# Decode attention with an FFN gate: 4-byte transposes, the FFN in column tiles in mid-stream, and a new order of loads

## Chip, cores and metric

The kernel runs on one core of one Trainium2 chip. The metric is the device time of one execution in microseconds. "Before" is the kernel as it stood, "after" the changed one. Runs differ in state: a run more than 1.5% above the fastest of the same kernel counts as slow. Ratios are the mean time of one kernel's fast runs over that of the other's of the same rounds, so they are not quite the ratio of the medians that I quote.

## The reference

Two batch rows, one new token each. The only large inputs are the last 2048 rows of the K and V caches (8 heads, 256 wide, 16 query heads), `wq`, `wo`, and the FFN's `w1` and `w2`.

```python
xn = layernorm(x)                                  # x: [2, 1, 448]
q  = (xn @ wq) as [2, 16 heads, 1, 256]
k, v = last 2048 rows of the caches, each of 8 heads used by 2 query heads
s  = softmax(q k^T / 16) v, as [2, 1, 4096] @ wo
g  = silu(relu(xn @ w1) @ w2)                      # w1: [448, 1792]
out = x + s * g                                    # bf16
```

## The kernel before

One pair is one of the 8 K/V heads for both batch rows: 2 MB of K and 2 MB of V (MB here is 2^20 bytes), in rows interleaved by batch over 128 partitions. A pair is cut into 8 steps. Step i transposes a chunk of K on TensorE into one of three PSUM banks, and VectorE (even i) or ScalarE (odd i) evacuates it, that is, copies it to SBUF. Scores, softmax and PV products (softmax weights times V) of earlier pairs stand between the steps.

```python
def do_T(i):                                       # one of 64 steps
    k, s = divmod(i, NCH)
    bank, src = tb[i % 3], kbuf[k % NKB]
    deps = [*d_k[k], p_id, evac.get(i - 3)]
    for n in range(8):
        lo = (4 * s + n % 4) * DH + 128 * (n // 4)
        o = pr.op(PE, lambda e, n=n, lo=lo: e.matmul(
            bank[:, n * 128:(n + 1) * 128], lhsT=src[:, lo:lo + 128], rhs=ident[:, :],
            start=True, stop=True, is_transpose=True), deps)
    ...
    if i % 2 == 0:
        evac[i] = pr.op(DVE, lambda e: e.tensor_copy(dst, bank[:, :]), deps)
    else:
        evac[i] = pr.op(ACTE, lambda e: e.activation(dst, bank[:, :], ACT.Copy), deps)

# pair k, e = 8k: scores at steps e+8, e+9; softmax e+9 to e+15 (row sum "ch_sum" at e+15);
# PV at e+17 to e+24; o_sb, oT after that.
# ... cut
order = ["v0"] + [n for k in range(2, NPAIR - 2) for n in (f"k{k}", f"v{k - 1}")]
order += ["k6", "k7", "v5", "v6", "v7"]            # k0, wq, k1 come first
# ... cut
load_w1(0)
load_w2(0)
# wo in four parts: 16, 10, 4, 2 of 32 slots; all the loads on one queue
do_H(0); do_H(1)                                   # h = relu(x w1): 2 x 7 products, 4 x 448 out
do_hT()
# ... at2: the attention output, folded for wo
do_F()                                             # h w2, then silu: ScalarE exp, VectorE 3 ops
# 128 products with wo, then out = x + s * g
```

Below, Kn and Vn are the K and V of pair n; H are the products with w1, hT the transposes of their result, F the products with w2. PE is TensorE, and a "row sum" is the small product `ch_sum`: that of one pair's softmax closes the next pair's transposes, so row sums mark TensorE's pace.

## Time and profile before

| | before |
|---|---|
| median, range | 115.96 us, 115.94 to 118.28 (3 runs) |
| profiled run | 118.03 us, span 114.7 us, slow |
| moved | 44.3 MB (decimal), 386 GB/s over the span |
| TensorE, VectorE, ScalarE busy | 74%, 41%, 40% |
| transposes (bf16, 512) | 42.0 us busy |

The page cuts the span into 40 slices; a digit is a busy share in tenths. The chain of waits lists what ended last, in time order, as start, duration, what. A full DMA row tells that transfers never stop; it does not tell that they set the end. For that, look at the last lines of the chain. Here TensorE stands there. The lines themselves are in the prediction below.

### The profile page before, as it was taken

The page shows a single profiled execution, that of the slowest core. Times are in us where ns is not written, and L with a number is a line of the kernel's source. Part 1 is how long each engine was busy: PE and PEld are TensorE (multiplying, and loading weights), DVE is VectorE, ACT ScalarE, POOL GpSimd, SP SyncE. Part 2 cuts the span into 40 slices and gives each one's busy share as a digit, 9 for nine tenths or more (in the row PEclk, how much of TensorE's full clock was granted, in tenths as well). Part 3 has the DMA queues.
Part 4 walks back from the last instruction along what each step waited for, and adds up shares of the span by engine and source line. Part 5 has one row for each costly group of instructions (what it writes and reads, how often), then busy time and mean ns, then how long its engine had stood idle before and what let it go on. Part 6 is the DMA issues. An engine that isn't in the chain of part 4 may idle for free.

```text
span 114.7 us, 2834 instructions
## 1 busy us (share of the span) xinstructions
PE 85.0 (74%) x1262; PEld 56.1 (49%) x1262; DVE 46.6 (41%) x123; ACT 45.7 (40%) x56; POOL 1.8 (2%) x13
## 2 busy tenths in 40 slices
PE   0009906089569989986998996799899858777890
PEld 0009902056444765753576574466576525212870
DVE  2633503025422636633454754464574513222231
ACT  1903630006953493490358358168358140000000
POOL 6000000000000000000000000000000000000000
PEclk9999999959976999998599999999999995555559
DMA  4899989999999999999999999999999999999300
GB/s 92 366 434 480 450 373 434 383 457 446 388 446 446 383 446 440 400 434 440 400 431 428 411 434 423 428 423 417 440 417 411 415 415 417 451 402 401 133 0 3
DMA packets 3744, 44.28 MB, mean 386 GB/s; under 512 B 659, under 2 KB 789, under 8 KB 1173
## 3 DMA queue, kind: packets, MB, share of 16 engines
q1 hardware_dynamic: 3704, 44.11, 91.7%
q8 instruction: 9, 0.15, 0.5%
q14 instruction: 3, 0.02, 0.0%
q10 hardware_dynamic: 28, 0.00, 0.0%
HBM read 44.11 MB, written 0.00 MB: 384 GB/s over the span
## 4 chain that ended last, share of the span: by engine, by line
PE 43%; DMA 41%; DVE 5%; SPq 4%; issue 3%; ACT 1%
DMA kbuf<-in_A_k_cache_dram 41%; PE tb L268 16%; PE sbk L249 8%; PE obk L249 7%; PE fbk L249 6%; PE mbk L249 6%; SPq L36 4%; DVE o_sb L353 1%; DVE h_n L400 1%; ACT e_sb L318 1%; DVE pt L330 1%; PE mbk L304 1%; DVE rm L299 1%; DVE tmp L496 0%; DVE out_sb L498 0%
## 5 line engine op out<-in xcount | busy, mean ns | idle before, releaser
L268 PE MATMUL tb<-ident,kbuf 128*128 128x128 bf16 x512 | 42.0, 235 | 9.1 <-issue 5.9
L281 ACT ACTIVATE kt<-tb 128x1024 bf16<-128x1024 bf16 x32 | 31.8, 1021 | 38.9 <-PE tb L268 38.9
L268 PEld LDWEIGHTS tb<-ident,kbuf 128*128 128x128 bf16 x512 | 33.4, 105 | 16.4 <-issue 14.0
L279 DVE COPY kt<-tb 128x1024 bf16<-128x1024 bf16 x32 | 22.1, 690 | 23.6 <-PE tb L268 23.5
L249 PE MATMUL obk<-vbuf,pt 128*4 128x256 bf16 x256 | 17.8, 295 | 0.0
L318 ACT ACTIVATE e_sb<-sbk,bias 128x1024 bf16<-128x1024 f32 x8 | 8.9, 1114 | 7.2 <-DVE bias L314 7.1
L249 PE MATMUL sbk<-kt,qz 128*4 128x512 bf16 x128 | 11.7, 443 | 0.0
L249 PEld LDWEIGHTS obk<-vbuf,pt 128*4 128x4 bf16 x256 | 6.0, 86 | 6.1 <-issue 0.6
L299 DVE TENSOR_REDUCE rm<-sbk 128x1 f32<-128x512 f32 x8 | 5.5, 692 | 7.8 <-PE sbk L249 7.8
L249 PE MATMUL fbk<-w_sb,xr 128*4 128x448 bf16 x14 | 5.5, 572 | 0.7 <-DVE h_n L400 0.7
L420 ACT ACTIVATE ea<-fbk 128x112 f32<-128x112 f32 x1 | 0.3, 263 | 14.4 <-PE fbk L249 14.4
L249 PE MATMUL mbk<-ssum,gsum 128*128 128x1 f32 x16 | 3.3, 273 | 3.1 <-DVE pt L330 1.9
L330 DVE TENSOR_TENSOR pt<-mbk,par 128x128 bf16<-128x128 f32 x8 | 2.3, 292 | 6.5 <-PE mbk L249 6.5
L353 DVE TENSOR_SCALAR o_sb<-obk,rs 128x256 bf16<-128x256 f32 x8 | 3.9, 484 | 2.3 <-PE obk L249 2.3
L249 PE MATMUL mbk<-ident,e_sb 128*128 128x16 bf16 x64 | 2.9, 171 | 2.4 <-ACT e_sb L318 2.4
L249 PEld LDWEIGHTS mbk<-ssum,gsum 128*128 128x128 f32 x16 | 2.6, 203 | 3.8 <-DVE pt L330 3.8
L249 PE MATMUL mbk<-ident,xg 2*128 2x2 bf16 x7 | 0.3, 163 | 5.5 <-DVE xg L228 5.5
L249 PEld LDWEIGHTS mbk<-ident,e_sb 128*128 128x128 bf16 x64 | 2.1, 96 | 3.5 <-ACT e_sb L318 2.8
L249 PE MATMUL obk<-wqo,xr 128*4 128x512 bf16 x28 | 1.7, 379 | 2.7 <-DMA wqo<-in_A_wq_dram 2.7
L249 PE MATMUL sbk<-wqo,at 128*2 128x112 bf16 x128 | 3.4, 297 | 0.2 <-issue 0.2
L249 PEld LDWEIGHTS fbk<-w_sb,xr 128*4 128x4 bf16 x14 | 1.5, 115 | 4.0 <-issue 2.5
L400 DVE TENSOR_SCALAR h_n<-fbk 4x448 bf16<-4x448 f32 x2 | 1.2, 612 | 5.3 <-PE fbk L249 5.3
(61 smaller groups left out, 43.8 us busy)
## 6 DMA issues: line engine op xcount, KB each, us to landing
kbuf<-in_A_k_cache_dram SPq DMA_DIRECT2D x16, 1024.0 KB, 19.9
vbuf<-in_A_v_cache_dram SPq DMA_DIRECT2D x16, 1024.0 KB, 22.6
wqo<-in_A_wq_dram SPq DMA_DIRECT2D x1, 3584.0 KB, 14.9
w_sb<-in_B_w_dram SPq DMA_DIRECT2D x2, 1568.0 KB, 22.5
wqo<-in_A_wo_dram SPq DMA_DIRECT2D x1, 1792.0 KB, 27.9
wqo<-in_A_wo_dram SPq DMA_DIRECT2D x1, 1120.0 KB, 30.2
wqo<-in_A_wo_dram SPq DMA_DIRECT2D x1, 448.0 KB, 29.9
wqo<-in_A_wo_dram SPq DMA_DIRECT2D x1, 224.0 KB, 30.0
```

What stands on the lines that cost most here:

```text
L36: o = _Op(eng, lambda e: e.dma_start(dst, src), [d for d in deps if d is not None], True)
L249: return lambda e: e.matmul(out_ap, lhsT=lhsT, rhs=rhs, start=start, stop=stop, skip_group_check=True, **kw)
L268: o = pr.op(PE, lambda e, n=n, lo=lo: e.matmul(bank[:, n * 128:(n + 1) * 128], lhsT=src[:, lo:lo + 128], rhs=ident[:, :], start=True, stop ...
L279: evac[i] = pr.op(DVE, lambda e: e.tensor_copy(dst, bank[:, :]), deps)
L281: evac[i] = pr.op(ACTE, lambda e: e.activation(dst, bank[:, :], ACT.Copy), deps)
L299: st["rm", k] = pr.op(DVE, lambda e: e.tensor_reduce(out=rm[k % 2][:, :], in_=sbk[:, :], axis=AX.X, op=ALU.max), [st["S", k], st.get(("rmT ...
L304: st["rmT", k] = pr.op(PE, lambda e: e.matmul(mbk_ap(0, 128, 1), lhsT=rm[k % 2][:, :], rhs=ident_f[:, :], start=True, stop=True, is_transp ...
L318: st["exp", k] = pr.op(ACTE, lambda e: e.activation(view(e_sb[k % 2], 0, [[2, 512], [1, 2]]), view(sbk, 0, [[1, 512], [0, 2]]), ACT.Exp, b ...
L330: st["pt", k] = st["mbk"] = pr.op(DVE, lambda e: e.tensor_tensor(out=view(pt[k % NP], 0, [[4, 32], [2, 2], [1, 2]]), in0=view(mbk, 256, [[ ...
L353: st["osb", k] = pr.op(DVE, lambda e: e.tensor_scalar(out=o_sb[k % 2][:, :], in0=obk[k % 2][:, 0:DH], scalar1=rs[:, k:k + 1], scalar2=None ...
L400: st["h_n"] = pr.op(DVE, lambda e: e.tensor_scalar(out=h_n[0:4, u * (FC // 2):(u + 1) * (FC // 2)], in0=fbk[0:4, 0:FC // 2], scalar1=0.0, ...
L420: a_e = pr.op(ACTE, lambda e: e.activation(ea[:, :], fbk[:, 0:NCOL], ACT.Exp, scale=-1.0), [o])
```

## The change

It has four parts. (1) K is transposed as 4-byte elements, half as many products, and the evacuation sorts the result by batch and parity with a strided read. (2) The FFN is computed in four column tiles and in pair 5 instead of in the tail. (3) w1 and w2 are loaded among the K/V pairs, k7 behind v5, wo last. (4) The first K pair comes in halves on two queues, with x behind it. The intent is to take the FFN out of the tail and halve the count of transposes.

```diff
+        d_k[0] = {}
+        for h in range(2):
+            for b in range(2):
+                lo = h * (NT // 2) * DH
+                d_k[0][h, b] = pr.dma((SP, ACTE)[b] if h == 0 else SP, ...)
+        d_x = pr.dma(ACTE, x_sb[0:B, :], A_x[:, 0, :])      # was first
...
-            for n in range(8):
-                lo = (4 * s + n % 4) * DH + 128 * (n // 4)
+            for n in range(4):
+                lo = (4 * s + n) * (DH // 2)
                 o = pr.op(PE, lambda e, n=n, lo=lo: e.matmul(
-                    bank[:, n * 128:(n + 1) * 128], lhsT=src[:, lo:lo + 128], rhs=ident[:, :],
+                    bank_f[:, n * 128:(n + 1) * 128], lhsT=src_f[:, lo:lo + 128], rhs=ident_f[:, :],
...
-                evac[i] = pr.op(DVE, lambda e: e.tensor_copy(dst, bank[:, :]), deps)
+                evac[i] = pr.op(DVE, lambda e: e.tensor_copy(dst, view(bank, 0, [[1, 4], [4, 256]])), deps)
             else:                                           # ScalarE likewise
...
-                o = pr.op(PE, mm(fbk[0:4, 0:FC // 2], xr[:, 4 * s:4 * s + 4], w1_sb[:, lo:lo + FC // 2], ...
+                for i in range(4):
+                    o = pr.op(PE, mm(fbk[32 * i:32 * i + 4, 0:256], xr[:, 4 * s:4 * s + 4],
+                                     view(w1_sb, s * FC + min(2 * i, 5), [[7, 128], [1, 2]]),
+                                     s == 0, s == SLOTS - 1, tile_position=(0, 32 * i)), deps)
...
+        at_step(5 * NCH + 2, 6, do_H)
+        at_step(5 * NCH + 4, 6, do_hT)
+        at_step(5 * NCH + 6, 6, do_F)
...
-        order += ["k6", "k7", "v5", "v6", "v7"]
+        for n in "v0 k2 v1 k3 v2 w1 k4 v3 w2 k5 v4 k6 v5 k7 v6 v7".split():
```

More of the change, by code (lines that the diff above doesn't have):

```diff
@@ L142, in bass_recurrent_scan__sliding_block_cached__dense_activation_relu__decode_kernel @@
         qz = named("qz", [128, 16 * NPAIR], BF)
-        h_n = named("h_n", [128, FC], BF)
+        h_n = named("h_n", [128, 256], BF)
         h_sb = named("h_sb", [128, 28], BF)
@@ L182, in kv_dst @@
             return view(t, 0, [[1, NT * DH]], n=64, p0=b, pstep=2)
-        d_x = pr.dma(ACTE, x_sb[0:B, :], A_x[:, 0, :])
         p_xc = pr.op(POOL, lambda e: e.memset(x_c[:, :], 0.0))
-        d_xc = [pr.dma(ACTE, view(x_c, 0, [[1, NCOL]], n=4, p0=b, pstep=32),
-                       A_x[b, 0, :].rearrange("(i n) -> i n", i=4), [p_xc]) for b in range(B)]
         d_k, d_v = {}, {}
@@ L202, in load_v @@
                       for b in range(2)]
-        load_k(0)
+        d_k[0] = {}
+        for h in range(2):
+            for b in range(2):
+                lo = h * (NT // 2) * DH
+                d_k[0][h, b] = pr.dma((SP, ACTE)[b] if h == 0 else SP,
+                                      view(kbuf[0], lo, [[1, NT // 2 * DH]], n=64, p0=b, pstep=2),
+                                      kv_src(0, b, A_k_cache)[:, lo:lo + NT // 2 * DH])
+        d_x = pr.dma(ACTE, x_sb[0:B, :], A_x[:, 0, :])
+        d_xc = [pr.dma(ACTE, view(x_c, 0, [[1, NCOL]], n=4, p0=b, pstep=32),
+                       A_x[b, 0, :].rearrange("(i n) -> i n", i=4), [p_xc]) for b in range(B)]
         d_wq = pr.dma(SP, wqo[:, 0:SLOTS * HC], wq_src)
@@ L250, in mm, with do_xr @@
                                       skip_group_check=True, **kw)
-        for s in range(SLOTS):
-            m_xr = pr.op(PE, mm(mbk_ap(2 * s, 2), xg[0:B, 128 * s + 128:128 * s + 256], ident[0:B, 0:B], s == 0),
-                         [v_xn, p_id])
-        v_xr = pr.op(DVE, lambda e: e.tensor_tensor(
-            out=view(xr, 0, [[4, SLOTS], [2, 2], [1, 2]]), in0=view(mbk, 0, [[2, SLOTS], [0, 2], [1, 2]]),
-            in1=view(par8, 0, [[1, SLOTS], [1, 2], [0, 2]]), op=ALU.mult), [m_xr, v_par8])
+        def do_xr():
+            for s in range(SLOTS):
+                m_xr = pr.op(PE, mm(mbk_ap(2 * s, 2), xg[0:B, 128 * s + 128:128 * s + 256], ident[0:B, 0:B], s == 0),
+                             [v_xn, p_id])
+            st["xr"] = pr.op(DVE, lambda e: e.tensor_tensor(
+                out=view(xr, 0, [[4, SLOTS], [2, 2], [1, 2]]), in0=view(mbk, 0, [[2, SLOTS], [0, 2], [1, 2]]),
+                in1=view(par8, 0, [[1, SLOTS], [1, 2], [0, 2]]), op=ALU.mult), [m_xr, v_par8])
         evac, last_S, freed = {}, {}, set()
@@ L264, in do_T @@
             bank, src = tb[i % 3], kbuf[k % NKB]
-            deps = [*d_k[k], p_id, evac.get(i - 3)]
-            for n in range(8):
-                lo = (4 * s + n % 4) * DH + 128 * (n // 4)
+            src_f, bank_f = src[:, :].bitcast(F32), bank[:, :].bitcast(F32)
+            landed = [d_k[0][s // 4, b] for b in range(2)] if k == 0 else d_k[k]
+            deps = [*landed, p_idf, evac.get(i - 3)]
+            for n in range(4):
+                lo = (4 * s + n) * (DH // 2)
                 o = pr.op(PE, lambda e, n=n, lo=lo: e.matmul(
-                    bank[:, n * 128:(n + 1) * 128], lhsT=src[:, lo:lo + 128], rhs=ident[:, :],
+                    bank_f[:, n * 128:(n + 1) * 128], lhsT=src_f[:, lo:lo + 128], rhs=ident_f[:, :],
                     start=True, stop=True, is_transpose=True), deps)
@@ L278, in do_T @@
             if i % 2 == 0:
-                evac[i] = pr.op(DVE, lambda e: e.tensor_copy(dst, bank[:, :]), deps)
+                evac[i] = pr.op(DVE, lambda e: e.tensor_copy(dst, view(bank, 0, [[1, 4], [4, 256]])), deps)
             else:
-                evac[i] = pr.op(ACTE, lambda e: e.activation(dst, bank[:, :], ACT.Copy), deps)
+                evac[i] = pr.op(ACTE, lambda e: e.activation(dst, view(bank, 0, [[1, 4], [4, 256]]), ACT.Copy), deps)
         def do_S(k, b):
@@ L289, in do_S @@
                     o = pr.op(PE, mm(sbk[32 * i:32 * i + 4, :], lhsT,
-                                     view(kt[(ch // 2) % (NKT // 2)], 512 * dhi + b, [[1024, 2], [2, 256]]),
+                                     view(kt[(ch // 2) % (NKT // 2)], 256 * (2 * b + dhi), [[1024, 2], [1, 256]]),
                                      b == 0 and dhi == 0, b == 1 and dhi == 1, tile_position=(0, 32 * i)),
@@ L370, in do_q @@
         def do_q():
-            deps = [d_wq, v_xr, a_z[0]]
+            deps = [d_wq, st["xr"], a_z[0]]
             for s in range(SLOTS):
@@ L380, in do_q @@
                 out=q_n[:, :], in0=obk[0][:, :], scalar1=SCALE, scalar2=None, op0=ALU.mult), [o])
-            deps = [v, v_xr]
+            deps = [v, st["xr"]]
             for n in range(4):
                 o = pr.op(PE, lambda e, n=n: e.matmul(
-                    mb16[:, 128 * n:128 * n + 128], lhsT=q_n[:, 128 * n:128 * n + 128],
+                    mb16[:, 128 * n:128 * n + 128], lhsT=view(q_n, 256 * (n // 2) + n % 2, [[2, 128]]),
                     rhs=ident[:, :], start=True, stop=True, is_transpose=True), deps)
@@ L391, in do_q, with do_H @@
                         view(mb16, 256 * r + b, [[2, 2], [32, 4], [128, 2]])), [o, p_qz])
-        def do_H(u):
-            deps = [st["w1"], a_z[3], st.get("h_n")]
+        def do_H():
+            deps = [st["w1"], st["xr"], a_z[3]]
             for s in range(SLOTS):
-                lo = s * FC + u * (FC // 2)
-                o = pr.op(PE, mm(fbk[0:4, 0:FC // 2], xr[:, 4 * s:4 * s + 4], w1_sb[:, lo:lo + FC // 2],
-                                 s == 0, s == SLOTS - 1), deps)
-                deps = []
+                for i in range(4):
+                    o = pr.op(PE, mm(fbk[32 * i:32 * i + 4, 0:256], xr[:, 4 * s:4 * s + 4],
+                                     view(w1_sb, s * FC + min(2 * i, 5), [[7, 128], [1, 2]]),
+                                     s == 0, s == SLOTS - 1, tile_position=(0, 32 * i)), deps)
+                    deps = []
             st["h_n"] = pr.op(DVE, lambda e: e.tensor_scalar(
-                out=h_n[0:4, u * (FC // 2):(u + 1) * (FC // 2)], in0=fbk[0:4, 0:FC // 2],
+                out=view(h_n, 0, [[1, 128], [128, 2]]), in0=view(fbk, 0, [[2, 128], [1, 2]]),
                 scalar1=0.0, scalar2=None, op0=ALU.max), [o])
@@ L405, in do_hT @@
             deps = [st["h_n"]]
-            for j in range(7):
-                o = pr.op(PE, mm(fbk[:, 4 * j:4 * j + 4], view(h_n, j, [[7, 128]], n=4), ident[0:4, 0:4], j == 0), deps)
+            for jj in range(2):
+                o = pr.op(PE, mm(fbk[:, 256 + 16 * jj:272 + 16 * jj], h_n[:, 128 * jj:128 * jj + 128],
+                                 view(ident, 0, [[32, 4], [1, 4]]), True, True), deps)
                 deps = []
+            for jj in range(2):
+                st["hT"] = pr.op(DVE, lambda e, jj=jj: e.tensor_copy(
+                    view(h_sb, 2 * jj, [[4, 3], [14, 2], [1, 2]]), view(fbk, 256 + 16 * jj, [[4, 3], [2, 2], [1, 2]])), [o])
             st["hT"] = pr.op(DVE, lambda e: e.tensor_copy(
-                view(h_sb, 0, [[2, 7], [14, 2], [1, 2]]), view(fbk, 0, [[4, 7], [2, 2], [1, 2]])), [o])
+                view(h_sb, 12, [[14, 2], [1, 2]]), view(fbk, 284, [[2, 2], [1, 2]])), [o])
         def do_F():
@@ L439, in bass_recurrent_scan__sliding_block_cached__dense_activation_relu__decode_kernel @@
             at_step(i, 0, lambda i=i: do_T(i))
+        at_step(2, 1, do_xr)
         at_step(NCH - 1, 1, do_q)
+        at_step(5 * NCH + 2, 6, do_H)
+        at_step(5 * NCH + 4, 6, do_hT)
+        at_step(5 * NCH + 6, 6, do_F)
         for k in range(NPAIR):
@@ L454, in bass_recurrent_scan__sliding_block_cached__dense_activation_relu__decode_kernel @@
             at_step(e + 25, 5, lambda k=k: do_oT(k))
-        order = ["v0"] + [n for k in range(2, NPAIR - 2) for n in (f"k{k}", f"v{k - 1}")]
-        order += ["k6", "k7", "v5", "v6", "v7"]
         loads = []
-        for n in order:
-            load, nb = (load_k, NKB) if n[0] == "k" else (load_v, NVB)
-            loads.append((load, int(n[1]), nb))
+        for n in "v0 k2 v1 k3 v2 w1 k4 v3 w2 k5 v4 k6 v5 k7 v6 v7".split():
+            if n[0] == "w":
+                loads.append(((load_w1, load_w2)[int(n[1]) - 1], 0, 1))
+            else:
+                load, nb = (load_k, NKB) if n[0] == "k" else (load_v, NVB)
+                loads.append((load, int(n[1]), nb))
         for i in range(max(steps) + 1):
@@ L468, in bass_recurrent_scan__sliding_block_cached__dense_activation_relu__decode_kernel @@
         assert not loads
-        load_w1(0)
-        load_w2(0)
         d_wo = []
@@ L476, in bass_recurrent_scan__sliding_block_cached__dense_activation_relu__decode_kernel @@
             j0 += n
-        do_H(0)
-        do_H(1)
-        do_hT()
         for b in range(2):
@@ L485, in bass_recurrent_scan__sliding_block_cached__dense_activation_relu__decode_kernel @@
                 view(at2, b, [[2, 32]]), mbk_ap(256 + 32 * b, 32)), [m_at])
-        do_F()
         deps = [v_at2, st["exp", NPAIR - 1]]
```

## The prediction

> **What bounds it now.** I first read the page's slices. The DMA row stands at 9 from the third slice to the 37th, so all but the ends is a full transfer stream; the TensorE clock falls to half for the last seven slices.
>
> ```profile
> PE   0009906089569989986998996799899858777890
> PEclk9999999959976999998599999999999995555559
> DMA  4899989999999999999999999999999999999300
> ```
>
> The table of windows says how steady the stream is, and where it ends: 421 to 434 GB/s through the middle, a ragged end, nothing after 109 us.
>
> ```profile
> 72.00:82.00 10.00, 9.20 (x147) 6.11 (x147) 5.24 (x13) 5.08 (x6) 0.00 (x0) 1.00 1.01 426
> 82.00:92.00 10.00, 9.30 (x153) 6.10 (x146) 5.61 (x17) 5.08 (x6) 0.00 (x0) 1.00 1.01 425
> 108.00:109.00 1.00, 1.00 (x54) 1.00 (x49) 0.25 (x2) 0.26 (x1) 0.00 (x0) 0.50 0.05 16
> ```
>
> So the stream moves 44.1 MB, a 1.05 MB half pair of K or V every 2.45 us, from about 3 us to 108.4 us: the last piece of wo was issued at 78.35 us and took 30.0 us to land. But the end is not set by it alone. The chain of waits shows only TensorE and the softmax from 70.8 us on, and at its end the FFN at half clock:
>
> ```profile
> 80.61 0.38 PE mbk L249 x2
> ...
> 89.04 0.38 PE mbk L249 x2
> ...
> 98.91 2.72 PE fbk L249 x7
> ...
> 102.32 2.79 PE fbk L249 x7
> ...
> 110.93 0.90 PE sbk L249 x20
> ```
>
> The first two lines are the same place (the row sum) one K/V pair apart: 8.43 us, the pace of TensorE when it is the limit. A pair's transfers take 4 x 2.45 = 9.8 us. Thus TensorE is slightly faster than DMA, and the end is two limits close together: the FFN (98.9 to 106.7 us) and then wo's products, which for a moment wait for wo's last pieces. DMA alone would end at 108.4 + 0.35 (last 8 products) + 2.9 (two vector operations, the output's transfer) = 111.7; the span is 114.7. The run traced was a slow one, 118.03 us, 3.3 over its span; the fast ones are 115.95, so a fast span is some 112.6, only 1 us above that floor.
>
> [...] a 128x128 bf16 load shows 98 ns, an f32 one 181 to 189. [...] here it went to 0.50 at 94.6 us after the softmax waits at 91 to 94 us. [...] The evacuation's 690 ns for 1024 elements is 1.5 elements a ns[...]. [...] Issues here take 0.6 us for 1 MB that needs 2.45 us.
>
> **Part 1, 4-byte transposes.** 512 of 128x128 bf16 become 256 f32.
>
> ```profile
> 84.63 0.28 PE L249 MATMUL obk<-vbuf,pt 128*4 128x256 bf16 x4
> 84.84 0.27 PE L304 MATMUL mbk<-ident_f,rm 128*1 128x128 f32 x1
> 84.95 0.61 PE L268 MATMUL tb<-ident,kbuf 128*128 128x128 bf16 x8
> ```
>
> The bf16 step of 8 runs from 84.08 (timeline) to 84.63: 0.55 us, that is 8 x 0.055 plus about 0.1 of switch. The existing f32 transpose streams the same 128 columns, and the next instruction follows 0.11 us later[...]. [...] If, as in bf16, the next load runs under the present product, a new step is 4 x 0.107 + 0.107 for the first, exposed load + 0.09 switch = 0.63 us. So halving the count saves nothing: **+0.08 a step, +0.63 a pair**, 9.06 us. The score products stay: their four column tiles already take 0.22 per 512 columns, so step 2 costs nothing now and step 1 saves nothing.
>
> VectorE's copy reads with a step of 4 elements[...]. A pair has 4, with 2.3 us of other work 7.2 us, still under 9. ScalarE (1.02 us[...]) should stay.
>
> **Part 2, FFN to pair 5.** Out of the tail go 98.9 to 106.7, 7.8 us. In column tiles H is 28 products of 256 columns, 7 x 0.107; hT two; F 14 x 0.047 at full clock. With switches 2.0 us, now between the transposes of pair 5, where vector work rises by 2.4 us too. w1 and w2 (3.2 MB, 7.5 us) move ahead of k4 and k5.
>
> **Part 3, order of loads.** This is what I think decides. Before, K7 landed at 77.2 (issue 62.07 plus landing time), with v5 to v7, both w and wo, some 31 us, behind it: all the late attention hid there. Now only v6, v7 and wo are behind K7: 4 x 2.45 + 3.67 MB/0.429 = 18.3 us, so **K7 lands at 108.3 - 18.3 = 90.0**, K6 at 80.2, K5 at 70.4. What must follow K7:
> - TensorE reaches pair 7: K5 at 70.4 + 9.06 + 2.0 (FFN) = 81.5; + 9.06 = 90.5, just after K7 lands.
> - pair 7's transposes to the row sum of pair 6: before, 80.99 to 89.04 = 8.05; + 0.63 = 8.7, so 99.2.
> - from there S7, softmax, PV7, oT and at2: before, 89.04 to 98.91, with the last at_exp to 99.2 and 0.9 for two fold products and copies not hidden behind the FFN: to 100.1, so 11.1 us. 110.3.
> - wo, 128 products at half clock, 3.2 us (128 x 25 ns); all of wo has landed by then. 113.5.
> - 2.9 to the end: **116.4**, and + 3.3 = 119.7 in a run like the one traced.
> The tail is compute, not transfer, again: what the FFN gave back (7.8), the later K7 takes (TensorE's row sum comes at 99.2 instead of 89.0, 10.2).
>
> **Part 4, start.** The first half of K0 lands near 6 us instead of 8.4 with the rest; x comes behind a K half on its queue, so the norm starts some 3 to 4 us later. Both are hidden: q needs wq at 16.9 us and pair 1 needs K1 at about 23. I count 0.
>
> **Rivals.**
> A: the DMA floor. If 4-byte loads and streams cost half of what I read[...], a step is about 0.32, a pair 6.6; row sum near 96, wo's products start at 107.1 and the span ends at 113.3, time 116.6: the same. Even a perfect tail cannot beat 111.7, time 115.0, 0.8% faster, unless the stream itself ends sooner. For it: the change's author wants fewer products. Against: the f32 row above.
> B: load and product of 4 bytes do not overlap: 0.88 a step, 11.1 a pair. TensorE falls behind DMA from pair 5 on; three pairs at +2 us more each, end at 122 to 123, time 125 to 126. Against: bf16 loads do overlap.
> C: VectorE becomes the limit through its long copies, in pair 5 above all (7.2 + 2.4 = 9.6): +1 us.
> D: clock. Waiting 4 us for K5 after K4's work may halve the clock for one window, +1; or a tail at full clock gives 2 to 2.5 back (PV7, wo's products at half). The two states of before, 2.1 us apart, are perhaps this, in its FFN. If instead they are a transfer lag, fast runs of after lie near 117.7.
>
> **Range and chances.** Main line 117.7 to 119.7, A (a fifth) 116 to 117, B (a sixth) 122 or more; I put 118.6, which is +2.3% on 115.95, with 115.9 to 122.2. Faster by 2% (under 113.6) would need the stream to end over a us sooner: 0.05. The line at 118.27 cuts my main case: same 0.42, slower 0.53.
>
> **What would show it.** Right: DMA row at 9 until 108 us; f32 transposes starting 0.107 apart; the DVE copy at 1.2 us; no FFN after 90 us; K7 landing at 90; wo products after 109 with no wait for wo. Wrong if: transposes 0.055 apart (A) or over 0.2 (B); wo products waiting for wo at the end (DMA floor); ScalarE copies longer too, which would slow every pair; gaps in the DMA row, from buffers freed late; or full clock after 100 us.

## The result

After: 121.60 us median (121.32 to 121.83, 4 runs, all fast), before 116.64 in the same rounds. The ratio of fast runs is 1.0445, interval 1.035 to 1.0539: **slower**. It lies inside my range and near its upper end; I had 118.6.

The clock and DMA rows of after's page:

```profile
PEclk9999679859958999995589985999679999996555
DMA  3998999999999999999999999999999999970000
```

The stream is as full as before and runs out in the 36th slice, at 108 us. Four slices with nothing follow it, where before had two: the end is not the stream's. The clock row has more dips.

The groups that changed most, with count, busy time, mean of one in ns:

```profile
L277 PE MATMUL tb<-ident_f,kbuf 128*128 128x128 f32 x256 | 46.2, 317 | 19.3 <-issue 9.8
L288 DVE COPY kt<-tb 128x1024 bf16<-128x1024 bf16 x32 | 39.0, 1223 | 21.1 <-PE tb L277 20.9
L290 ACT ACTIVATE kt<-tb 128x1024 bf16<-128x1024 bf16 x32 | 32.0, 1021 | 44.9 <-PE tb L277 44.9
```

The same groups before:

```profile
L268 PE MATMUL tb<-ident,kbuf 128*128 128x128 bf16 x512 | 42.0, 235 | 9.1 <-issue 5.9
L281 ACT ACTIVATE kt<-tb 128x1024 bf16<-128x1024 bf16 x32 | 31.8, 1021 | 38.9 <-PE tb L268 38.9
L279 DVE COPY kt<-tb 128x1024 bf16<-128x1024 bf16 x32 | 22.1, 690 | 23.6 <-PE tb L268 23.5
```

Half the transposes take as long as all did. VectorE's copy went from 690 to 1223 ns, ScalarE's stayed at 1021.

The chain of waits of after, cut to its joints:

```profile
67.60 2.55 issue
70.15 0.63 PE tb L277 x4
...
79.05 0.16 DVE bias L323
...
79.23 1.21 ACT e_sb L327 x2
80.43 0.91 ACT kt L290
81.35 0.16 ACT ea L434
...
81.79 0.86 DVE tmp L437
...
82.95 0.21 DVE pt L339
...
83.20 0.38 PE mbk L255 x2
...
93.32 0.38 PE mbk L255 x2
...
98.43 1.23 DVE kt L288
99.66 0.08 DVE bias L323
...
100.96 1.84 ACT kt L290 x2
...
111.80 0.23 PE mbk L255 x2
...
113.36 3.19 PE sbk L255 x128
```

K5's two DMAs land at 67.60 and 70.06 us (the wait for the second stands as issue) and from there no transfer stands in the chain again. Pair 5 lasts until the row sum at 83.20, pair 6 until 93.32. In pair 5 the silu (`ea`, `tmp`) sits on VectorE in front of `pt`, which TensorE needs. In pair 7 a long VectorE copy (98.43) is followed by `bias`, `exp` and two ScalarE copies before the last scores. wo's products start at 113.36 and run 3.19 us without a wait: all of wo landed at 108.3.

### The profile page after: what moved, and what is told of

It reads as the page before. It is cut to its first block, busy times and chain, and to the rows that moved or that the text cites.

```text
span 119.6 us, 2338 instructions
## 1 busy us (share of the span) xinstructions
PE 85.6 (72%) x1015; PEld 53.5 (45%) x1015; DVE 62.9 (53%) x124; ACT 45.6 (38%) x56; POOL 1.8 (2%) x13
## 4 chain that ended last, share of the span: by engine, by line
DMA 43%; PE 34%; DVE 6%; ACT 5%; SPq 5%; issue 3%
DMA kbuf<-in_A_k_cache_dram 43%; PE tb L277 14%; PE sbk L255 9%; PE obk L255 5%; SPq L36 5%; PE mbk L255 4%; ACT e_sb L327 3%; ACT kt L290 2%; PE fbk L255 1%; DVE o_sb L362 1%; DVE kt L288 1%; PE mbk L313 1%; DVE tmp L437 1%; DVE pt L339 1%; DVE rm L308 1%
## 5 line engine op out<-in xcount | busy, mean ns | idle before, releaser
L277 PE MATMUL tb<-ident_f,kbuf 128*128 128x128 f32 x256 | 46.2, 317 | 19.3 <-issue 9.8
L288 DVE COPY kt<-tb 128x1024 bf16<-128x1024 bf16 x32 | 39.0, 1223 | 21.1 <-PE tb L277 20.9
L277 PEld LDWEIGHTS tb<-ident_f,kbuf 128*128 128x128 f32 x256 | 32.7, 161 | 27.5 <-issue 23.0
L255 PE MATMUL obk<-vbuf,pt 128*4 128x256 bf16 x256 | 18.5, 303 | 0.0
L255 PE MATMUL sbk<-kt,qz 128*4 128x512 bf16 x128 | 13.3, 490 | 0.2 <-ACT kt L290 0.2
L255 PEld LDWEIGHTS sbk<-kt,qz 128*4 128x4 bf16 x128 | 2.1, 80 | 4.0 <-issue 3.5
L347 DVE RECIPROCAL rs<-mbk 128x1 f32<-128x1 f32 x8 | 1.3, 169 | 3.8 <-PE mbk L255 3.8
L255 PE MATMUL mbk<-one_f,mrow 1*128 1x1 f32 x16 | 3.0, 256 | 0.3 <-DVE mrow L316 0.2
L255 PEld LDWEIGHTS mbk<-fold,o_sb 128*128 128x128 bf16 x16 | 1.0, 103 | 4.9 <-DVE o_sb L362 3.1
L255 PEld LDWEIGHTS sbk<-wqo,at 128*2 128x2 bf16 x128 | 2.9, 124 | 0.4 <-DVE at L498 0.4
```

The costliest lines, as they stand in the source:

```text
L255: return lambda e: e.matmul(out_ap, lhsT=lhsT, rhs=rhs, start=start, stop=stop, skip_group_check=True, **kw)
L277: o = pr.op(PE, lambda e, n=n, lo=lo: e.matmul(bank_f[:, n * 128:(n + 1) * 128], lhsT=src_f[:, lo:lo + 128], rhs=ident_f[:, :], start=True ...
L288: evac[i] = pr.op(DVE, lambda e: e.tensor_copy(dst, view(bank, 0, [[1, 4], [4, 256]])), deps)
L347: st["rs", k] = st["mbk"] = pr.op(DVE, lambda e: e.reciprocal(rs[:, k:k + 1], mbk_ap(130, 1)), [st["gs", k]])
```

## The experiments

Twelve kernels. I name the theory T: after is slow because K5 to K7 land later with the same dependent work behind them, on a TensorE path that cannot catch up. Rivals: the transposes and strided copies (R1), the silu in the engines' queues (R2), the start (R3).

### Part 3 alone on before

```diff
-order += ["k6", "k7", "v5", "v6", "v7"]; w1, w2 behind v7
+"v0 k2 v1 k3 v2 w1 k4 v3 w2 k5 v4 k6 v5 k7 v6 v7"
```

> The kernel before with only the new order of loads (part 3 alone: w1 and w2 ahead of k4 and k5, k7 behind v5); its 2-byte transposes, its plain start and its untiled FFN in the tail stay. Theory (what costs is that K6 and K7 land 7.5 and 12.6 us later with the same work behind them): row sum before the last scores near 98.5 instead of 89.0, the FFN of 8 us still behind it, so 8 to 10 us slower: 124 to 127. Rival (the stream has slack, the order of equal bytes does not matter): within 1% of before.

Measured: 123.86 us median (122.71 to 126.77, 3 runs, the longest slow), ratio 1.0564 (1.0451 to 1.0677). The order alone costs about as much as the whole change, or more; the two intervals overlap. Its chain of waits:

```profile
98.09 0.38 PE mbk L249 x2
...
107.30 2.29 PE fbk L249 x7
...
110.28 1.50 PE fbk L249 x7
...
115.61 1.45 issue
117.06 0.57 PE sbk L249 x29
```

The row sum before the last scores came at 98.09 instead of 89.04; I had written 98.5. Bytes, products and durations are those of before: only the place of K, w1 and w2 changed. Here TensorE did wait for K7: by the trace's records it landed at 89.81, and pair 7's transposes start at 89.90, though TensorE had ended pair 6 at 89.24. The loss was some 6.6 us and not 8 to 10 because here part of the FFN ran at full clock (1.50 against 2.79 us for the second half of H). T's mechanism stands. The 1.45 us is no wait for wo, whose last piece had landed at 108.35: TensorE stopped with 29 products left, while wo's parts end with 24 and 8 left. In before it stopped at the same product, for 0.23 us at 110.70. Here the trace has a 16 KB instruction transfer from 114.57 to 115.72. So I think that TensorE ran out of instructions; this is argued, not tested.

### k7 ahead of v5, in after

```diff
-w2 k5 v4 k6 v5 k7 v6 v7
+w2 k5 v4 k6 k7 v5 v6 v7
```

> The changed kernel with k7 loaded ahead of v5, w1 and w2 still early; K7 lands 4.9 us earlier, near 85. Theory: no change (121 to 122), since TensorE only comes to pair 7 at 93.5 us, 3.7 us after K7 lands at 89.7; what matters is K5 at 70 us and the work behind it. Rival (K7's landing is the limit, as my prediction's list put it): 3 to 4 us faster, 118.

Measured: 121.47 us (121.31 to 121.88, 4 runs), ratio to before 1.0414 (1.0343 to 1.0484); after's own was 1.0445. K7 landed at 85.0 instead of 89.7 and nothing moved: the row sum that ends pair 6 came at 93.51 instead of 93.32. So K7's own landing is not the limit in after; the delay is made earlier, from K5's landing on. (No run brings K5 alone forward: that it is K5 is read from the chain.) In my prediction's list K7's landing and TensorE's arrival fell together (90.0 and 90.5); measured, TensorE comes 3.6 us after K7.

### Parts 2 and 3 undone in after

```diff
-        at_step(5 * NCH + 2, 6, do_H) ... do_hT ... do_F
-order "v0 k2 v1 k3 v2 w1 k4 v3 w2 k5 v4 k6 v5 k7 v6 v7"
+order "v0 k2 v1 k3 v2 k4 v3 k5 v4 k6 k7 v5 v6 v7 w1 w2"; do_H, do_hT, do_F in the tail
```

> The changed kernel with parts 2 and 3 undone: loads in before's order (k6, k7 ahead of v5; w1, w2 after v7) and the FFN, still in column tiles, in the tail. The new transposes and the new start stay. Theory: K6 lands at 72.3 and K7 at 77.2 again; the column-tiled FFN takes some 4 us of the tail instead of 7.8; the end is then the transfer stream's (108.3 + 3.3 = 111.7 span, time 113.5 to 115), faster than before by 1 to 2%. Rival 1 (transposes): stays above 118.5. Rival 2 (start): the same as rival 1.

Measured: 115.17 us (114.34 to 116.15, 20 runs, one of them slow), ratio 0.9899 (0.9872 to 0.9926). With the transposes, the strided copies, the new start and the column tiles all kept, 6.4 us come back. The chain:

```profile
106.31 1.99 PE sbk L255 x90
108.29 0.64 issue
108.93 0.67 PE sbk L255 x37
```

wo's products stop at 108.29 with 37 left, in the middle of one of wo's parts. An instruction transfer had ended at 107.73, as in the run above. wo's last piece landed at 108.40, so even without that stop the end could have come only some 0.8 us earlier: the stream's end and TensorE's are that close now, and both are far from the 113.36 at which after only starts. R1 and R3 alone cannot carry the loss.

### Part 1 undone in after

```diff
-            for n in range(4):   # 4-byte, with the strided evacuation and the q and score views
+            for n in range(8):   # as before
```

> The changed kernel with the 2-byte transposes and plain evacuation copies of before (part 1 undone, all else kept). Theory (the loss comes from K5 to K7 landing late and from TensorE's path behind them, not from the transposes): TensorE is the limit over about three pairs, each 0.25 to 0.3 us cheaper, so about 0.7 to 1 us faster than the changed kernel's 121.6: 120.6 to 121. Rival 1 (the strided vector copies and 4-byte products cause the loss): back to 116 to 117.5.

Measured: 118.95 us (118.66 to 119.22, 4 runs), ratio 1.0262 (1.0201 to 1.0324). That is 2.65 us faster than after, against 0.7 to 1 expected: **my expectation missed**. Part of it is the pair. Where TensorE is the limit and the clock is full, a pair takes 8.66 us in after (93.32 to 101.98, both row sums) and 8.44 here (91.00 to 99.44). Three pairs give 0.7. In the last pair the scores wait another 0.5 us for ScalarE's copies in after and not here. The rest is the clock, see below.

### Part 1 alone on before

```diff
-            for n in range(8):   # 2-byte
+            for n in range(4):   # 4-byte, with the strided evacuation and the q and score views
```

> The kernel before with only the 4-byte transposes and the strided evacuation (part 1 alone). Theory: two to three pairs at +0.25 us each, so 0.5 to 1 us slower than before, under 1%. Rival 1: 3 us or more slower, 2.5% or more.

Measured: 117.07 us (115.48 to 119.89, 20 runs), before 116.37 (39 runs), ratio of fast runs 1.0025 (0.9985 to 1.0065). On before the transposes cost at most 0.7%. I take it that what they cost depends on how long TensorE has nothing else to wait for: two pairs there, three in after.

### The silu moved out of pair 5

```diff
 def do_F():
     ... # 56 products
-    a_e = ...exp; v_d; v_rc; st["g"]
+    st["F"] = o                      # exp and the three VectorE ops now stand behind at2, in the tail
```

> The changed kernel with the silu of the FFN (one ScalarE exp, three VectorE operations) moved behind the last attention step; everything else kept. Theory: in pair 5 the trace shows TensorE waiting from 79.0 to 83.2 us while the pt product stands behind the silu on VectorE and the silu's exp behind an evacuation on ScalarE; without it about 2.5 us come back and the time is about 119. Rival (TensorE waits for K7 anyway, or the wait only moves): no change, 121 to 122.

Measured: 119.86 us (119.22 to 120.05, 4 runs), ratio 1.0323 (1.0263 to 1.0384): 1.74 us better, less than the 2.5 I expected. And its trace shows another way than the one I had in mind. Pair 5 ended only 0.3 us earlier, at 82.91, in a run whose half clock at K5 lasted until 75.1 us instead of 74.3. The gain is in pair 6, 8.6 us instead of 10.1. The table of windows tells why; the windows are 3.41 us, the grid of the clock's own records, and the columns are length, then busy time and count of PE, PEld, DVE, ACT and POOL, then the granted clock. First after:

```profile
81.10:84.51 3.41, 2.02 (x32) 1.20 (x30) 2.10 (x6) 1.31 (x3) 0.00 (x0) 1.00 1.01 428
84.51:87.92 3.41, 3.41 (x30) 1.73 (x22) 2.08 (x5) 1.02 (x1) 0.00 (x0) 0.50 1.00 423
```

Then the kernel with the late silu:

```profile
81.92:85.33 3.41, 3.03 (x43) 1.81 (x46) 1.96 (x4) 1.44 (x3) 0.00 (x0) 1.00 1.03 437
```

And the one with the old transposes, whose silu still waits:

```profile
80.10:83.50 3.40, 2.44 (x73) 1.86 (x62) 2.04 (x7) 1.79 (x3) 0.00 (x0) 1.00 1.04 439
83.50:86.90 3.40, 3.40 (x59) 1.96 (x52) 2.56 (x6) 1.23 (x2) 0.00 (x0) 1.00 0.99 414
```

In after, TensorE is busy 2.02 of 3.41 us, and in the next window the clock is at half. Pair 6 then takes 10.1 us and not 8.66: 1.4 us. With 3.03 or 2.44 us busy the clock stays full, in the window after them too. The run with k7 early shows the same half window (84.86 to 88.28 us) as after. So the wait for the silu costs once where it stands and once more in the window after it, and the long 4-byte steps and copies add to it. That these traces agree is measured; each is one profiled run.

The busy time of that table is no threshold, though: before's window 70.71 to 74.12 has 2.09 us and is followed by full clock, after_old_transposes' window 100.58 to 103.99 has 2.41 and is followed by half. A recount of all fourteen traces sorts them. A product's record runs on past its stream: a bf16 transpose is recorded 0.219 us long, and the next one starts 0.055 after it. So take 0.164 us off the end of each record and count the rest, transposes included. Of the 278 windows at full clock that start between 17 and 112 us, 63 are followed by half clock, with at most 1.60 us of 3.41 by this count, and 215 by full clock, with at least 1.64. After's window has 1.48, the run with k7 early 1.49, the old transposes 1.80, the late silu 2.36. This was found in the traces afterwards; no run was made to test it, and four windows before 17 us do not fit.

### Old transposes and late silu together

```diff
+ both edits above, on after
```

> The changed kernel with both the old transposes and the silu moved behind the last attention step; order of loads, FFN products in pair 5 and the new start stay. Theory (TensorE is the limit from K5's landing on, so savings there add until it waits for K7 at 89.7 us): the old transposes gave 2.65 us, the late silu 1.85; together 3 to 4 us, less than the sum because TensorE would come to pair 7 before K7 has landed: 117.5 to 118.5. Rival (one of the two carries the other): no better than the old transposes alone, 118.9.

Measured: 118.34 us (118.11 to 118.48, 4 runs), ratio 1.0151 (1.0095 to 1.0206). The two gains are 2.65 and 1.74 us alone and 3.3 together. They share the half window of pair 6, as the traces say: neither kernel had it. TensorE came to pair 7 at about 91.6 us and K7 had landed at 89.6, so it was still not waiting for K7 (the expectation's reason for the shortfall did not come true).

### Part 4 alone on before

```diff
-load_k(0); x first on the ScalarE queue; xr before step 0
+K0 in halves on two queues, x behind; do_xr at step 2
```

> The kernel before with only the new start (first K pair in halves on two queues, x behind it, xr in step 2; part 4 alone). Theory: within 0.3% of before, since the stream starts at the same time and pair 1 waits for K1 at 22 to 23 us either way. Rival (an earlier start of the transposes moves everything): 1 us or more faster.

Measured: 116.38 us (115.64 to 118.03, 12 runs), before 116.30, ratio 0.9969 (0.9927 to 1.0012). No effect, as expected.

### Column tiles alone on before

```diff
-do_H(0); do_H(1)     # 14 products of 4 x 448
+do_H()               # 28 products of 256 columns in four column tiles, still in the tail
```

> The kernel before with only the column tiles of the FFN, left in the tail. Theory: the FFN's 7.8 us in the tail become some 5.4 (as in the run with the FFN in the tail: 1.6 + 1.3 + 1 + 1.4), then wo's products wait for the last piece of wo at 108.3 us: the end is the stream's, 115 (1.2% faster than before), the same as with the new transposes. Rival (new transposes or new start did the good there): 116 to 116.5.

Measured: 115.02 us (114.97 to 115.68, 6 runs), ratio 0.9866 (0.9812 to 0.9921). The useful piece of part 2 is the tiling, not the place.

### Column tiles, w1 and w2 between v6 and v7, FFN where TensorE waits for v7

```diff
-order += ["k6", "k7", "v5", "v6", "v7"]; w1, w2 behind
+... k6 k7 v5 v6 w1 w2 v7; do_H and do_hT at step 72, do_F at step 73
```

> As the last, but w1 and w2 land between v6 and v7 and the FFN runs while TensorE waits for v7; k6 and k7 stay early. Nothing of the FFN is then behind v7. Theory: attention's last products wait for v7 (99.6), wo's first products start near 103 and its last ones wait for the last piece of wo: the stream's end again, 114.5 to 115.2. If it were a good deal faster than before_ffn_columns, TensorE and not the stream had set the end there.

Measured: 114.92 us (114.78 to 115.02, 6 runs), ratio 0.9847 (0.9795 to 0.9898). Against the last kernel nothing is gained, so TensorE had not set the end there. The chain ends in a wait for wo:

```profile
109.72 0.04 issue
109.76 0.30 PE sbk L249 x8
```

wo's last piece landed at 109.72, 1.4 us later than in before. The trace's completion records say why. The trace has 16 of them for a load, which I take for one from each of the page's 16 DMA engines; here are those of the last part of wo, in us after the first one (made from the trace's records, not a view of the profile):

```
before (first at 106.58)            0.00 0.13 0.14 0.16 0.17 0.24 0.31 1.06 1.58 1.60 1.62 1.64 1.69 1.70 1.71 1.76
before_ffn_columns (106.61)         0.00 0.08 0.13 0.14 0.17 0.19 0.20 1.01 1.52 1.54 1.59 1.63 1.67 1.69 1.72 3.17
before_ffn_hidden (106.63)          0.00 0.02 0.04 0.13 0.17 0.18 0.26 1.22 1.52 1.53 1.54 1.56 1.65 1.67 1.68 3.09
after_ffn_hidden (106.60)           0.00 0.07 0.12 0.14 0.25 0.27 0.30 0.38 1.25 1.64 1.64 1.75 1.76 1.80 1.82 1.84
```

In the first 20 us of before_ffn_hidden all 16 engines agree within 0.28 us. At 20.6 us the trace has a 16 KB transfer of the kind "instruction", and in the next load one engine is 1.58 us late; at 37.0 another, and a second engine is 1.56 late; and so on, one engine more for each such transfer (46.9, 56.7, 66.6, 76.4, 86.0, 94.5); one of 8 KB at 57.6 makes another 1.2 us late. The engines are still as late at the stream's end (1.52 to 1.68 us in the table); that they cannot catch up because the stream has no gap is my reading, not tested. The transfer at 104.6 us fell on an engine that was late already: 3.1 us.

### The same on after

```diff
-order and FFN steps of after
+... k6 k7 v5 v6 w1 w2 v7; do_H and do_hT at step 72, do_F at step 73
```

> The changed kernel with k6 and k7 early again and the FFN between v6 and v7 (w1, w2 loaded there): the new transposes and start kept, the rest as in before_ffn_hidden. Theory: the end is the stream's last piece of wo, 108.4 us where no instruction fetch falls on the lagging DMA engine near the end, 109.7 where it does (both runs with old transposes had one at 104.6 and 106.0 us); span 111.7 to 113, time 114 to 115. Rival (the new transposes slow the tail): 116 or more.

Measured: 113.62 us (113.49 to 114.65, 6 runs), ratio 0.976 (0.971 to 0.9809). wo's last piece landed at 108.44 and none of its records is later than 1.84. It beats both kernels.

### New transposes in before_ffn_hidden, and nothing else

```diff
 before_ffn_hidden
-            for n in range(8):   # 2-byte
+            for n in range(4):   # 4-byte, with the strided evacuation and the q and score views
```

> before_ffn_hidden with the 4-byte transposes of the change and nothing else of it (the old start stays). It lies between before_ffn_hidden (114.92) and after_ffn_hidden (113.62), which differ in transposes and start and ran on different chips. Theory: the 1.3 us between them are an instruction fetch: with 2-byte transposes a late fetch falls a second time on one DMA engine, whose last piece of wo lands 3.1 us after the first engine's; with 4-byte ones there are 496 instructions fewer, two fetches fewer, and it lands 1.8 us after. So 113.5 to 113.8, last landing 108.4. Rival (the new start or the chip made the difference): 114.8 to 115.

Measured: 113.61 us (113.49 to 114.56, 6 runs), ratio 0.9707 (0.9658 to 0.9755). The last landing was at 108.34. The same edit that cost after 2.65 us gains 1.3 here, against before_ffn_hidden's 114.92 on another chip. The program has 2340 instructions and 8 instruction transfers within the traced time instead of 2853 and 10, and no engine is hit twice before the end. (That is 513 fewer; the 496 that I expected is the difference of before and after.) That fewer instructions, and not another property of the 4-byte form, is what moved the second hit is argued from these records; I did not pad a program with idle instructions to show it alone. With the same ratio to before within the intervals, this and after_ffn_hidden are the best versions I have.

## Why the prediction was right or wrong

**The bound before** was read rightly: TensorE close to DMA, and the end some 2 to 3 us over the stream's. But the floor in time was off: I added 3.3 us, one slow run's difference of time and span, and so called 115.0 the best that a perfect tail could do; after_ffn_hidden, with a span of 111.8, took 113.62. The fastest of the 39 runs of before beside the first experiments have spans of 113.5 to 113.8 and times 2.1 above them; after's four runs lie 1.8 to 1.9 above theirs. The fast span of before was thus 113.5 and more, not the 112.6 that I worked out. Two lines were read a little loosely: the DMA row has an 8 in its sixth slice, and the clock is at half in six of the last seven slices (0.50 from 94.6 to 111.7 us; that the softmax waits of 91 to 94 us did it is read from the order in time).

**Part 1**, in itself: right in two figures. The timeline of after shows products 0.109 us apart (starts at 90.351, 90.461, 90.570), for the 0.11 read in before, and the copy takes 1.22 us (mean 1223 ns), the 1.2 of my list. That 1.2, and with it the 7.2 and 9.6 us of VectorE's work, was an estimate of mine that no trace of before shows. The 0.107 of an exposed load was an estimate too, from the two loads of one_f, which start 0.108 us apart in before (85.697 and 85.805). The first load exposes 0.056, so a step is 0.585, not 0.63, and a pair 8.66, not 9.06. But I treated it as a fixed toll of a pair. With its copies in pair 5 and in the last softmax it cost 2.65 us in the changed kernel.

**Part 2**, the step that failed: "With switches 2.0 us, now between the transposes of pair 5". From K5's start to the next pair it was 13.4 us (70.15 to 83.58), not 11.1 (70.4 to 81.5). H took 1.44 us (75.00 to 76.43), not 0.75: its groups of four run 0.20 us apart at full clock. The silu held `pt` until 82.95; TensorE sat idle 1.39 us there, 0.38 without the silu. And pair 5 began at half clock after the wait for K5, which I had among the rivals (D, "+1"): in before_new_order, with no FFN in pair 5, that pair takes 10.5 us (70.27 to 80.80) instead of 8.43, so it is 2.1 there, with half clock until 74.86. In after it ended at 74.27: some 1.6 us, an estimate in the same proportion. Pair 6 lost another 1.4 to the half window that the silu's wait left. I gave both no place in the main line.

**Part 3** was right: the order decides. Row sum at 98.09 against the 98.5 expected of the run that has it alone, and there the wait for K7 (landed 89.81) was the point. In the changed kernel "K7 lands at 90.0" was right (89.7) and not the point, as the early k7 showed: TensorE was already later than that.

**The tail** was right in size: 11.4 us from the row sum to wo's products for 11.1, wo 3.19 for 3.2, 3.05 to the end for 2.9. The clock was at half from 108.40 us to the end, and there was no wait for wo. **Part 4** was right: 0.

**Rivals.** A and B are refuted by the spacing of 0.109. C came true in a form that I did not describe: not VectorE's sum of busy time, but one operation in front of another. And the short wait that I read in before's chain as one for wo's last pieces (110.93) was not that, as before_new_order showed. The sum: main line 116.4 of span, measured 119.6, so 3.2 us missing, nearly all in pairs 5 and 6; the smaller difference to the time gave 1.5 back. And I had put 118.6, in the middle of my main line, where its upper end of 119.7 was nearer. That 121.6 lies in my range is partly luck: it is above the main line and below B's 122, in none of the cases that I worked out, and the range covered it because B, which did not happen, had stretched it to 122.2.

## What to carry to other kernels

In a full transfer stream the order of equal bytes was worth microseconds (6.6 us in before_new_order): load first what has the longest chain of work behind it (here K, then V, then weights whose work is short and free of order), and leave last only what is consumed in a fraction of a microsecond (wo's last 8 products took 0.30 us in before_ffn_hidden). When work is moved into the middle of a tight pipeline, follow its operations through the queue of every engine (in after `pt` stood behind the silu on VectorE until 82.95 us), and look at the clock window after any wait that it makes (in after half clock from 84.51 to 87.92 us); here moving the silu away gave 1.74 us back, beside some 2.3 us that the moved products themselves take. Once the stream sets the end, look at the 16 engines one by one: a last record at 3.09 us instead of 1.84 went with 114.92 instead of 113.62 us.

## Figures from these traces

- 4-byte transposes: 128 f32 columns took 0.109 us in after (90.351 to 90.461) against 0.055 for 128 bf16 columns in before, with the loads hidden but for 0.056 us at the first of a group, so that half the count saved nothing: 46.2 us busy for 256, 42.0 for 512.
- The clock: windows that were far from idle were followed by half clock. After's had 2.02 of 3.41 us busy by the records, 1.48 by the recount above, which puts the border in these traces between 1.60 and 1.64.
- Strided moving operand: H's, pairs of bf16 elements 14 bytes apart, ran 0.20 us for each group of four 256-column products at full clock (after, from 75.00 us), where the groups of PV's contiguous 256 columns start 0.108 apart (after, 105.809 and 105.917). Before's scores read with a step of 2 elements and took 0.22 us for 512 columns, as long a column as PV's.
- The stream: 2^20 bytes in 2.45 us, 428 GB/s, and 421 to 434 GB/s in before's windows from 42 to 92 us.
- Instruction transfers: before has eight of 16 KB ahead of the last landing, and eight of wo's last 16 records are 1.58 to 1.76 us late; in after it is six, at 1.53 to 1.82. A second hit went with 3.09 us in before_ffn_hidden. TensorE stopped for 0.23 us in before (110.70), 0.64 in after_ffn_tail (108.29) and 1.45 in before_new_order (115.61); I read that as a want of instructions, and no run tests it.
- Strided write: H's result in after, 128x256 elements from f32 PSUM with a step of 128 on the way out, took 1318 ns, where the o_sb scaling of the same size takes 480.
